# Decoding doubles with a two-slope activation, and a new table of engines and ranks, in an attention-plus-MLP kernel

## The chip, the cores and the metric

The kernel runs on one core of one Trainium2 chip. The metric is the device time of one execution in microseconds; a kernel's time is the median of several runs. In the text PE is TensorE, DVE is VectorE, ACT is ScalarE, POOL is GpSimd and SP is SyncE, whose queue issues all DMAs here.

## The reference

Causal attention over 4 batches, 12 heads, 448 positions and 64 channels; its output, as 1792 rows of 768, goes through a two-layer MLP.

```
scores = np.matmul(q, k.transpose(0, 1, 3, 2)) / np.sqrt(64)
scores = np.where(mask, -1000000000.0, scores)         # mask: above the diagonal
attn = np.exp(scores - np.max(scores, axis=-1, keepdims=True))
attn = attn / (np.sum(attn, axis=-1, keepdims=True) + 1e-09)
x = np.matmul(attn, v).transpose(0, 2, 1, 3).reshape(1792, 768)
h = x @ w_in                                            # w_in 768 x 2048
out = ((h - np.tanh(h)) @ w_out).astype(np.float32)     # w_out 2048 x 768
```

The two weight matrices arrive as 8-byte floats. The result has to be close to what float32 would give, while the matrix products run on 16-bit numbers. So every operand is scaled by a power of two and split into a high and a low float16 half, and each product is made of three: high by high, high by low, low by high.

## The kernel before, in words

**An operation recorded, then placed.** Nothing is issued when it is written. `Engine` hands each operation to `Work.add`, which notes its reads and writes; `Work.schedule` (line 166) then lists all operations in one order, by a rank that each carries (`rank(...)`, from the table `RANK`) and by the planner's own prices, and `Work.emit` issues them. Every instruction of the trace therefore has line 232. Some operations have two or three forms, one for each engine that can do them: `Work.either` takes the engine from a string of the table `CFG`, letter by letter in turn ("AVV": ACT, DVE, DVE, and again). Within an engine the order is fixed when the program is built.

**Front: weights, and the first 128 rows of each batch.** `w_in_chunk` takes one of 8 blocks of 256 columns of `w_in`: two loads of 768 KB, two calls of `decode`, a bound on the magnitudes, and `split` into halves. `decode` makes float32 from an 8-byte float with integer work. ACT multiplies the upper word by 2^-112 into PSUM; a first DVE pass (SCALAR_TENSOR_TENSOR) shifts that left by 3 and ORs in three bits of the lower word, and a second ORs in the sign, which the shift had pushed out. The first pass leaves the magnitude in a scratch buffer of the tile `e`, and the bound is taken from there: for `w_in` by a matmul of those magnitudes with ones, for `w_out` by an ACT instruction Abs whose accumulator sums them. `w_out_half` does the same for two halves of 8 loads each, through two landing buffers. Meanwhile `first_rows` computes the attention of rows 0 to 127 of two batches at a time (chunks `c` and `c2`), and `mlp_g` the first MLP layer for them.

**Attention of the other 320 rows.** `attention(b)` goes over 6 pairs of heads; there are 24 pairs in all. For each pair `prep` loads q and k, takes a bound of each (`bound`, DVE TENSOR_REDUCE), and splits q, k and v into halves. `weights_unit` runs three times: score matmuls (18 for a pair), a DVE custom instruction that adds the mask and finds the row minimum (tile `prob`), ACT Exp, a reciprocal, and `split` of the 5 probability tiles of a pair into `pn` (high, then low); a DMA transposes `pn` to `pt` (three for a pair, one buffer for each of the three). `values` multiplies `pt` with v (54 matmuls), and `split_x` writes the halves of x.

**MLP.** For each block of 128 hidden columns `mlp1` issues 18 matmuls into one of two PSUM banks (`b_m`), ACT Tanh and a DVE subtraction write `t`, and `split` makes `g`. `mlp2` issues 48 matmuls for a block of 128 rows and half the columns, evacuates them to `o` and stores them. The MLP matmuls of a batch are placed between the attention matmuls of the next, so PE has them to fill its time with. What is left when attention ends is PE work alone.

`split` (line 410) is the place where engines trade: the high half is one multiplication (`scaled`: DVE, ACT or POOL), and the low half is one DVE instruction, or two on POOL (multiply in place, subtract).

Of the kernel before, what the change touches and what calls it, by code (L numbers as in the profile page):

```python
# [9 lines left out]
F32 = mybir.dt.float32  # L10
BF16 = mybir.dt.bfloat16
I16 = mybir.dt.int16
I32 = mybir.dt.int32
U16 = mybir.dt.uint16
I64 = mybir.dt.int64
AF = mybir.ActivationFunctionType
ALU = mybir.AluOpType
# [241 lines left out]
def attention_then_mlp(ctx, tc, qk, v, w_in, w_out, out):  # L259
# [13 lines left out]
    V, A, G, T, S = (Engine(wk, n) for n in "VAGTS")  # L273
# [5 lines left out]
    NCC = DM // P  # L279
# [32 lines left out]
    ones = buf([P, P], BF16, "ones")  # L312
# [16 lines left out]
    q16_ring = ring(3, [P, 2, SEQ1], F16, "q16")  # L329
# [67 lines left out]
    def bound(o, i, junk=None, tag=None):  # L397

        if junk is None:
            V.tensor_reduce(o, i, axis=AX.X, op=ALU.max, apply_absolute_value=True)  # L400
            return
        wk.either(tag, lambda: V.tensor_reduce(o, i, axis=AX.X, op=ALU.max, apply_absolute_value=True),
                  lambda: A.activation(junk, i, AF.Abs, accum_out=o))
# [15 lines left out]
    def decode(y, raw, t, tag):  # L419

        words = raw.rearrange("p a b -> p (a b)").bitcast(I32)
        lo, hi = words[:, 0::2], words[:, 1::2]
        yi = y.rearrange("p a b -> p (a b)").bitcast(I32)
        top = words.bitcast(U16)[:, 1::4]
        wk.either("shift" + tag, lambda: V.tensor_scalar(t, lo, 29, None, ALU.logical_shift_right),
                  lambda: A.activation(t, top, AF.Copy, scale=2.0 ** -13, bias=2.0 ** -14 - 0.5),
                  lambda: G.tensor_scalar(t, top, 2.0 ** -13, 2.0 ** -14 - 0.5, ALU.mult, ALU.add))
        for n in range(2):  # L430
            part = slice(n * NW // 2, (n + 1) * NW // 2)
            g = bank_w()[:, :NW // 2]
            A.activation(g, hi.bitcast(F32)[:, part], AF.Copy, scale=2.0 ** -112)
            V.scalar_tensor_tensor(t[:, part], g.bitcast(I32), 3, t[:, part], ALU.logical_shift_left, ALU.bitwise_or)
            V.scalar_tensor_tensor(yi[:, part], g.bitcast(I32), -2 ** 31, t[:, part], ALU.bitwise_and, ALU.bitwise_or)

    def scratch(i, n=4):
        return e_block.bitcast(I32)[:, (i % n) * NW:(i % n + 1) * NW]

    def w_in_chunk(j):  # L440
        y = view(TS[3 + j % 2], 0, [NCC, 256], F32)
        pm = bank_1[:, :256]
        mags = []
        for a in range(2):
            i = 2 * j + a
            t = view(TS[i % 3], 0, [3, 256], I64)
            rank(RANK["c0"] - 1 if i < CFG["early"] else RANK["w_in"])
            S.dma_start(t, w_in[a * 3 * P:(a + 1) * 3 * P, j * 256:(j + 1) * 256].rearrange("(c p) f -> p c f", p=P))
            rank(RANK["w_in"])
            decode(y[:, a * 3:(a + 1) * 3], t, scratch(i), "_in")  # L450

            mag = scratch(i).bitcast(BF16)[:, 1::2].rearrange("p (c f) -> p c f", c=3)
            mags += [mag[:, c] for c in range(3)]
        with wk.group():
            for cc in range(NCC):
                T.matmul(pm, ones, mags[cc], start=(cc == 0), stop=(cc == NCC - 1))
        acc, s = r_acc(), r_s1()
        V.tensor_reduce(acc, pm, axis=AX.X, op=ALU.max)
        scales(us_in[:, j:j + 1], s, acc, 1e-30)
        split(w_in16[j][:, 0], w_in16[j][:, 1], y, s, "w_in")  # L460
# [4 lines left out]
    def w_out_half(n):  # L465

        ys = [view(TS[m], 0, [4, HALF], F32) for m in ((1, 2, 3, 4), (5, 6, 7, 4))[n]]
        to = ([TS[0], TS[1], TS[2], TS[3]], [ES[1], TS[5], TS[6], TS[7]])[n]
        acc = acc_out[n]
        for m in range(4):  # L470
            for a in range(2):
                i = n * 8 + 2 * m + a
                t = view(ES[1 + i % 2], 0, [2, HALF], I64)
                f0 = (2 * m + a) * 2 * P
                S.dma_start(t, w_out[f0:f0 + 2 * P, n * HALF:(n + 1) * HALF].rearrange("(c p) e -> p c e", p=P))
                mag = scratch(i, 2)
                decode(ys[m][:, 2 * a:2 * a + 2], t, mag, "_out")
                A.activation(mag.bitcast(F32), mag.bitcast(F32), AF.Abs, accum_out=acc[:, 2 * m + a:2 * m + a + 1])
        a1, s = r_acc(), r_s1()
        V.tensor_reduce(a1, acc, axis=AX.X, op=ALU.max)  # L480
        bound_scale(us_out[:, n:n + 1], s, a1, 0, mx_w)
        V.tensor_scalar(s_out[n], rel_in, s, None, ALU.mult)
        for m in range(4):
            w_out16[n][m] = view(to[m], 0, [2, 4, HALF], F16)
            for a in range(2):
                part = slice(2 * a, 2 * a + 2)
                split(w_out16[n][m][:, 0, part], w_out16[n][m][:, 1, part], ys[m][:, part], s_out[n][:, 2 * m + a:2 * m + a + 1], "w_out")
# [161 lines left out]
    def prep(b, hp, vf, sv):  # L649

        kq = qk_ring()
        S.dma_start(kq, qk[b, hp, :, P:])
        kf, qf = kq[:, :SEQ], kq[:, SEQ:]
        o = Chunk()
        ma, m2, us, s, o.cn = r_ma(), r_m2(), r_us2(), r_s2(), r_cn()
        bound(ma[:, 0:1], qf)
        bound(ma[:, 1:2], kf)
        with wk.group():
            for i in range(2):
                over_partitions(ma[:, i:i + 1], 2 + i)  # L660
        V.tensor_reduce(m2, bank_1[:, 2 * P:].rearrange("p (i n) -> p i n", i=2), axis=AX.X, op=ALU.max)
        scales(us, s, m2, 1e-12)
        V.tensor_scalar(o.cn, us[:, 0:1], us[:, 1:2], -(D ** -0.5), ALU.mult, ALU.mult)
        o.k, o.q = k16_ring(), q16_ring()
        split(o.k[:, 0], o.k[:, 1], kf, s[:, 1:2], tag(b, "k"))
        split(o.q[:, 0], o.q[:, 1], qf, s[:, 0:1], tag(b, "q"))
        o.v16 = v16_ring()
        split(o.v16[:, 0], o.v16[:, 1], vf, sv, tag(b, "v"))
        return o
# [120 lines left out]
        wk.emit()  # L790


CFG = {"early": 4, "e_bufs": 5, "shift_in": "A", "inverse": "A", "w_in": "VGGG", "w_in_lo": "G", "shift_out": "A", "w_out": "VVG", "w_out_lo": "V", "p0": "G", "p0t": "AAAV", "x0": "AV", "g0": "AG", "g0_lo": "G", "g2": "AAGA", "g2_lo": "G", "g": "AVG", "g_lo": "V", "o": "A", "k_first": "V", "k_first_lo": "VGG", "q_first": "A", "q_first_lo": "GV", "v_first": "GV", "v_first_lo": "VGGG", "p_first": "AVA", "p_first_lo": "V", "k": "G", "k_lo": "G", "q": "VAV", "q_lo": "VG", "v": "V", "v_lo": "VG", "p": "AVV", "p_lo": "V", "x": "V"}
RANK = {"c0": -1.131, "w_in": 0.126, "evac": 5.148, "w_out": 5.279, "c0b": 5.008, "att0": 5.082, "att": -0.403}


_OUTS = [((1792, 768), "float32")]
# [27 lines left out]
```

## Time and profile before

| | |
|---|---|
| median of 3 runs | 637.21 us (636.11 to 638.82) |
| the profiled execution | 637.71 us, span 635.7 us from first to last instruction |
| mean granted clock of PE | 0.97 |
| busy: PE, DVE, ACT, POOL | 572.8, 481.1, 293.8, 231.2 us |

The span and the profiled execution differ by 2.0 us, which lie before the first and behind the last instruction. Busy time is the time in which at least one instruction of the engine runs. PE's is no measure of how full it is, because matmuls overlap each other: how many of them are done in a stretch is the better measure. The same holds in small for DVE, whose instructions begin a little before the one ahead has ended.

### The profile page before, as it was taken

The numbers are of one execution on the slowest core, as the hardware profiler recorded it, in microseconds if no ns is written. First come the engines' busy times: TensorE is split into PE (matmuls) and PEld (weight loads), VectorE is DVE, ScalarE is ACT, GpSimd is POOL, SyncE is SP. The second block draws the span as 40 slices with busy tenths as digits, with TensorE's granted clock in tenths as the row PEclk, the third lists the DMA queues.
The fourth block names the chain that finished last, engine by engine and source line by source line (L and its number), as shares of the span: only waits on it lengthen the run. The fifth ranks groups of instructions, "written<-read, shape, count | busy, mean of one in ns | idle before, by whom it ended". The sixth has DMA issues, their size and how long they took to land.

```text
span 635.7 us, 13502 instructions
## 1 busy us (share of the span) xinstructions
PE 572.8 (90%) x5144; PEld 379.5 (60%) x5144; DVE 481.1 (76%) x1407; ACT 293.8 (46%) x792; POOL 231.2 (36%) x260
## 2 busy tenths in 40 slices
PE   3567759999999987999899999999999999999997
PEld 3345538887555554666466666556656666676664
DVE  3999886998999999999797999991399970244000
ACT  6778869984156544645234444330355430132000
POOL 2579985795322425053243335040043410000000
PEclk9779769999999999999989999999999999999999
DMA  8996166655077864645845364772034351000100
GB/s 280 332 336 194 31 198 202 191 150 208 28 168 152 128 132 104 119 92 84 195 97 124 94 101 94 155 144 50 25 86 67 67 104 35 14 1 1 26 26 25
DMA packets 113665, 74.01 MB, mean 116 GB/s; under 512 B 90048, under 2 KB 99776, under 8 KB 113088
## 3 DMA queue, kind: packets, MB, share of 16 engines
q1 hardware_dynamic: 113600, 73.15, 46.5%
q8 instruction: 40, 0.66, 0.4%
q14 instruction: 25, 0.20, 0.1%
HBM read 45.61 MB, written 5.51 MB: 80 GB/s over the span
## 4 chain that ended last, share of the span: by engine, by line
PE 40%; DVE 37%; DMA 10%; ACT 6%; POOL 3%; issue 3%; SPq 0%; ACTq 0%; POOLq 0%; DVEq 0%
PE b_m L232 36%; DVE pn L232 8%; DVE small L232 7%; DVE prob L232 5%; DMA slot<-in_moe_w_in_dram 5%; DVE t L232 4%; DVE g L232 4%; DVE slot L232 3%; DMA e<-in_v_dram 3%; PE b_x L232 2%; ACT e L232 2%; DVE x L232 2%; PE b_s L232 2%; ACT b_s L232 2%; DVE v L232 1%
## 5 line engine op out<-in xcount | busy, mean ns | idle before, releaser
L232 PE MATMUL b_m<-x,w_in 128*128 128x320 f16 (+1 forms) x1728 | 233.5, 293 | 5.8 <-DVE t L232 4.0
L232 PEld LDWEIGHTS <-w_in 128*128 128x128 f16 x1728 | 167.4, 99 | 65.9 <-issue 16.7
L232 PE MATMUL b_m<-slot,g 128*128 128x384 f16 x1152 | 192.6, 327 | 0.0
L232 PEld LDWEIGHTS <-g 128*128 128x128 f16 x1152 | 111.1, 98 | 74.5 <-issue 3.1
L232 ACT ACTIVATE prob<-prob,small 128x256 f32<-128x256 f32 (+2 forms) x120 | 69.1, 576 | 87.7 <-DVE small L232 87.0
L232 DVE SCALAR_TENSOR_TENSOR t<-b_m,small,t 128x320 f32<-128x320 f32 (+1 forms) x96 | 50.1, 522 | 33.2 <-ACT t L232 33.1
L232 ACT ACTIVATE o<-b_m,small 128x384 f32<-128x384 f32 x28 | 16.1, 575 | 124.1 <-PE b_m L232 124.1
L232 DVE SCALAR_TENSOR_TENSOR pn<-prob,small,pn 128x256 f16<-128x256 f32 (+2 forms) x120 | 71.3, 621 | 0.2 <-ACT pn L232 0.2
L232 ACT ACTIVATE t<-b_m,small 128x320 f32<-128x320 f32 (+1 forms) x96 | 47.9, 499 | 48.4 <-PE b_m L232 44.1
L232 POOL TENSOR_SCALAR g<-t,small 128x320 f16<-128x320 f32 (+1 forms) x29 | 18.3, 630 | 139.9 <-DVE t L232 112.0
L232 DVE CUSTOM_DVE_ANT_0 prob<-b_s,mask,small 128x256 f32<-128x256 f32 (+1 forms) x96 | 50.3, 542 | 23.5 <-PE b_s L232 23.4
L232 PE MATMUL b_s<-k,q 64*128 64x384 f16 (+2 forms) x432 | 45.2, 317 | 12.3 <-DVE small L232 5.0
L232 POOL TENSOR_SCALAR slot<-slot,small 128x448 f32<-128x448 f32 (+3 forms) x37 | 35.8, 968 | 36.3 <-DVE slot L232 13.0
L232 DVE SCALAR_TENSOR_TENSOR g<-t,small,g 128x320 f16<-128x320 f32 x64 | 37.1, 585 | 8.1 <-ACT g L232 3.8
L232 ACT ACTIVATE pn<-prob,small 128x256 f16<-128x256 f32 (+2 forms) x50 | 28.2, 576 | 28.3 <-DVE small L232 27.5
L232 DVE SCALAR_TENSOR_TENSOR e<-b_s,e 128x384 int32<-128x384 int32 x64 | 34.5, 550 | 5.1 <-ACT b_s L232 4.6
L232 PEld LDWEIGHTS <-q 64*128 64x128 f16 (+1 forms) x432 | 18.5, 98 | 32.5 <-issue 20.1
L232 PEld LDWEIGHTS <-v 128*64 128x64 f16 x1296 | 32.4, 113 | 8.1 <-issue 8.1
L232 PE MATMUL b_x<-pt,v 128*64 128x128 f16 (+1 forms) x1296 | 35.6, 213 | 0.5 <-DMA pt<-pn 0.2
L232 DVE SCALAR_TENSOR_TENSOR slot<-b_s,e 128x384 int32<-128x384 int32 x64 | 34.6, 551 | 0.5
L232 DVE TENSOR_SCALAR pn<-prob,small 128x256 f16<-128x256 f32 (+2 forms) x70 | 34.5, 506 | 0.6 <-DMA pt<-pn 0.5
L232 PE MATMUL b_m<-slot,first 128*128 128x384 f16 x192 | 33.4, 326 | 0.0
(96 smaller groups left out, 723.0 us busy)
## 6 DMA issues: line engine op xcount, KB each, us to landing
slot<-in_moe_w_in_dram SPq DMA_DIRECT2D x16, 768.0 KB, 5.8
slot<-in_moe_w_out_dram SPq DMA_DIRECT2D x8, 768.0 KB, 4.8
e<-in_moe_w_out_dram SPq DMA_DIRECT2D x8, 768.0 KB, 4.5
slot<-in_qk_dram SPq DMA_DIRECT2D x16, 384.0 KB, 3.2
e<-in_v_dram SPq DMA_DIRECT2D x3, 1536.0 KB, 7.2
out_dram<-o SPq DMA_DIRECT2D x24, 192.0 KB, 1.9
qk<-in_qk_dram SPq DMA_DIRECT2D x8, 384.0 KB, 3.1
g<-in_qk_dram SPq DMA_DIRECT2D x6, 256.0 KB, 6.9
```

The lines of the kernel that those rows point to most:

```text
L232: getattr(self.eng[o["eng"]], method)(*args, **kw)
```

## The change

Three things change.

1. `decode`: ACT's multiplication by 2^-112 becomes Prelu, which scales negative numbers by a further 2^32. After the left shift by 3 such a number keeps its sign in the top bit. So the second DVE pass is dropped, and the one that stays writes the result itself.
2. Bounds. The magnitudes no longer exist in the scratch buffer. `w_in` gets an ACT Abs over the 1536 decoded columns of a chunk, written as bfloat16 to the buffer that will take the high half, and the matmul with ones reads that. The bound of `w_out` and those of q and k go through `bound`, with engines by turns: `b_out` "AAV", `b_qk` "VVA".
3. `CFG` and `RANK` have new values throughout. The ones that move most: the low half of the probabilities `p_lo` from "V" to "GV", `p` from "AVV" to "VA", `g_lo` from "V" to "GV", `g` from "AVG" to "A", `w_in_lo` from "G" to "V", `k` from "G" to "A", `q` from "VAV" to "AAG", `x` from "V" to "AV".

```diff
@@ decode
-            A.activation(g, hi.bitcast(F32)[:, part], AF.Copy, scale=2.0 ** -112)
-            V.scalar_tensor_tensor(t[:, part], g.bitcast(I32), 3, t[:, part], ALU.logical_shift_left, ALU.bitwise_or)
-            V.scalar_tensor_tensor(yi[:, part], g.bitcast(I32), -2 ** 31, t[:, part], ALU.bitwise_and, ALU.bitwise_or)
+            A.activation(g, hi.bitcast(F32)[:, part], AF.Prelu, scale=2.0 ** -112, alpha=2.0 ** 32)
+            V.scalar_tensor_tensor(yi[:, part], g.bitcast(I32), 3, t[:, part], ALU.logical_shift_left, ALU.bitwise_or)
@@ w_in_chunk
-            mag = scratch(i).bitcast(BF16)[:, 1::2].rearrange("p (c f) -> p c f", c=3)
-            mags += [mag[:, c] for c in range(3)]
+        acc, s = r_acc(), r_s1()
+        mag = w_in16[j][:, 0].bitcast(BF16)
+        A.activation(mag, y, AF.Abs)
+        pm = bank_1[:, :256]
         with wk.group():
             for cc in range(NCC):
-                T.matmul(pm, ones, mags[cc], start=(cc == 0), stop=(cc == NCC - 1))
-        acc, s = r_acc(), r_s1()
+                T.matmul(pm, ones, mag[:, cc], start=(cc == 0), stop=(cc == NCC - 1))
@@ w_out_half
-                A.activation(mag.bitcast(F32), mag.bitcast(F32), AF.Abs, accum_out=acc[:, 2 * m + a:2 * m + a + 1])
+                y = ys[m][:, 2 * a:2 * a + 2].rearrange("p a b -> p (a b)")
+                bound(acc[:, 2 * m + a:2 * m + a + 1], y, mag.bitcast(F32), "b_out")
@@ prep
-        bound(ma[:, 0:1], qf)
-        bound(ma[:, 1:2], kf)
+        o.k, o.q = k16_ring(), q16_ring()
+        bound(ma[:, 0:1], qf, o.q[:, 0].bitcast(BF16), "b_qk")
+        bound(ma[:, 1:2], kf, o.k[:, 0].bitcast(BF16), "b_qk")
...
-        o.k, o.q = k16_ring(), q16_ring()
@@ tables
-CFG = {"early": 4, "e_bufs": 5, "shift_in": "A", "inverse": "A", "w_in": "VGGG", "w_in_lo": "G", "shift_out": "A", "w_out": "VVG", "w_out_lo": "V", "p0": "G", "p0t": "AAAV", "x0": "AV", "g0": "AG", "g0_lo": "G", "g2": "AAGA", "g2_lo": "G", "g": "AVG", "g_lo": "V", "o": "A", "k_first": "V", "k_first_lo": "VGG", "q_first": "A", "q_first_lo": "GV", "v_first": "GV", "v_first_lo": "VGGG", "p_first": "AVA", "p_first_lo": "V", "k": "G", "k_lo": "G", "q": "VAV", "q_lo": "VG", "v": "V", "v_lo": "VG", "p": "AVV", "p_lo": "V", "x": "V"}
-RANK = {"c0": -1.131, "w_in": 0.126, "evac": 5.148, "w_out": 5.279, "c0b": 5.008, "att0": 5.082, "att": -0.403}
+CFG = {"early": 4, "e_bufs": 5, "b_out": "AAV", "b_qk": "VVA", "shift_in": "AGGG", "inverse": "VAAA", "w_in": "G", "w_in_lo": "V", "shift_out": "A", "w_out": "AAV", "w_out_lo": "V", "p0": "G", "p0t": "A", "x0": "A", "g0": "V", "g0_lo": "GVVG", "g2": "GV", "g2_lo": "G", "g": "A", "g_lo": "GV", "o": "VAA", "k_first": "AVV", "k_first_lo": "V", "q_first": "GAAA", "q_first_lo": "V", "v_first": "AGV", "v_first_lo": "GGVV", "p_first": "A", "p_first_lo": "VG", "k": "A", "k_lo": "GGGV", "q": "AAG", "q_lo": "V", "v": "V", "v_lo": "V", "p": "VA", "p_lo": "GV", "x": "AV"}
+RANK = {"c0": -0.453, "w_in": 0.64, "evac": 7.121, "w_out": 7.805, "c0b": 4.125, "att0": 4.883, "att": -1.096}
```

The order of instructions shows three places on which the prediction rests. The first is DVE in the first `w_in` chunk, with `e` the scratch, `slot` the decoded weights and `b_s` the PSUM bank that ACT writes. Before:

```order
L232 SCALAR_TENSOR_TENSOR e_74<-b_s_111,e_74 128x384
L232 SCALAR_TENSOR_TENSOR slot_69<-b_s_111,e_74 128x384
L232 SCALAR_TENSOR_TENSOR e_74<-b_s_112,e_74 128x384
L232 RECIPROCAL small_108<-small_108 128x4
L232 SCALAR_TENSOR_TENSOR slot_69<-b_s_112,e_74 128x384
```

And with the change:

```order
L232 RECIPROCAL small_108<-small_108 128x4
L232 SCALAR_TENSOR_TENSOR slot_69<-b_s_111,e_74 128x384
L232 SCALAR_TENSOR_TENSOR slot_69<-b_s_112,e_74 128x384
L232 RECIPROCAL small_108<-small_108 128x4
L232 SCALAR_TENSOR_TENSOR slot_69<-b_s_111,e_74 128x384
```

The pass into `e` is gone everywhere: 128 passes become 64. The second place is POOL where the attention of the first pairs begins, with `prob` the probabilities, `pn` their halves, and `v`, `q`, `k` the halves of those operands. Before:

```order
L232 TENSOR_SCALAR v_100<-x_85,small_108 128x512
L232 TENSOR_SCALAR x_85<-x_85,small_108 128x512
L232 TENSOR_TENSOR v_100<-x_85,v_100 128x512
L232 TENSOR_SCALAR qk_93<-qk_93,small_108 128x320
L232 TENSOR_TENSOR q_94<-qk_93,q_94 128x320
L232 TENSOR_SCALAR slot_70<-slot_70,small_108 128x448
L232 TENSOR_TENSOR k_98<-slot_70,k_98 128x448
```

And with the change:

```order
L232 TENSOR_SCALAR q_94<-qk_93,small_108 128x320
L232 TENSOR_SCALAR prob_102<-prob_102,small_108 128x256
L232 TENSOR_TENSOR pn_106<-prob_102,pn_106 128x256
L232 TENSOR_SCALAR prob_104<-prob_104,small_108 128x384
L232 TENSOR_TENSOR pn_106<-prob_104,pn_106 128x384
L232 TENSOR_SCALAR prob_101<-prob_101,small_108 128x256
L232 TENSOR_TENSOR pn_106<-prob_101,pn_106 128x256
L232 TENSOR_SCALAR prob_105<-prob_105,small_108 128x448
L232 TENSOR_TENSOR pn_106<-prob_105,pn_106 128x448
```

POOL gets half of the low halves of the probabilities, as pairs of instructions, which it did not touch before. The third place is DVE behind the scores of the last (24th) pair of heads, with `t` the hidden block of the MLP and `x` the attention output. Before:

```order
L232 SCALAR_TENSOR_TENSOR pn_106<-prob_105,small_108,pn_106 128x448
L232 TENSOR_SCALAR x_85<-b_x_113 128x320
L232 SCALAR_TENSOR_TENSOR x_85<-b_x_113,x_85 128x320
L232 TENSOR_SCALAR x_85<-b_x_113 128x320
L232 SCALAR_TENSOR_TENSOR x_85<-b_x_113,x_85 128x320
L232 SCALAR_TENSOR_TENSOR t_88<-b_m_114,small_108,t_88 128x320
```

And with the change:

```order
L232 SCALAR_TENSOR_TENSOR pn_106<-prob_105,small_108,pn_106 128x448
L232 TENSOR_SCALAR small_108<-small_108 128x2
L232 COPY small_108<-small_108 64x2
L232 SCALAR_TENSOR_TENSOR t_87<-b_m_114,small_108,t_87 128x320
L232 SCALAR_TENSOR_TENSOR t_88<-b_m_115,small_108,t_88 128x320
L232 SCALAR_TENSOR_TENSOR g_84<-t_88,small_108,g_84 128x320
L232 SCALAR_TENSOR_TENSOR t_86<-b_m_114,small_108,t_86 128x320
```

With the change the first MLP layer of the third batch stands behind the probabilities of the last pair: 32 blocks `t` follow them, where 16 did. On PE 576 first-layer and 582 second-layer matmuls follow the first scores of the last pair, where it was 306 and 480.

## Rows read from the trace of the kernel before

**Rows 1.** The page: busy us of each engine, and the chain that ended last.
```profile
PE 572.8 (90%) x5144; PEld 379.5 (60%) x5144; DVE 481.1 (76%) x1407; ACT 293.8 (46%) x792; POOL 231.2 (36%) x260
...
PE 40%; DVE 37%; DMA 10%; ACT 6%; POOL 3%; issue 3%; SPq 0%; ACTq 0%; POOLq 0%; DVEq 0%
```

**Rows 2.** Windows by stage: PE, PEld, DVE, ACT, POOL busy (count), clock, DMA share, GB/s.
```profile
20.00:100.00 80.00, 52.20 (x386) 37.63 (x387) 72.18 (x278) 61.98 (x164) 64.48 (x47) 0.79 0.66 214
100.00:176.00 76.00, 74.34 (x600) 57.47 (x598) 69.72 (x130) 47.08 (x100) 50.84 (x71) 1.00 0.48 152
176.00:513.50 337.50, 317.93 (x3239) 200.84 (x3237) 300.76 (x892) 149.67 (x438) 108.12 (x126) 0.99 0.53 108
513.50:635.70 122.20, 118.52 (x868) 76.16 (x866) 28.35 (x65) 21.72 (x46) 3.08 (x6) 1.00 0.10 27
```

**Rows 3.** Windows of two stretches within attention, same columns.
```profile
200.00:240.00 40.00, 36.63 (x436) 21.80 (x433) 39.92 (x129) 21.12 (x63) 12.54 (x14) 1.00 0.75 144
...
420.00:460.00 40.00, 40.00 (x350) 24.67 (x349) 13.66 (x44) 8.98 (x29) 6.09 (x7) 1.00 0.34 68
```

**Rows 4.** Windows behind attention: one with first-layer, one with second-layer matmuls alone.
```profile
560.00:580.00 20.00, 20.00 (x149) 14.40 (x148) 9.93 (x19) 5.90 (x11) 1.59 (x3) 1.00 0.01 2
...
600.00:620.00 20.00, 20.00 (x126) 12.04 (x124) 0.00 (x0) 1.74 (x3) 0.00 (x0) 1.00 0.10 30
```

**Rows 5.** Groups by form (busy us, mean ns; then idle before): decode, and halves of weights.
```profile
L232 DVE SCALAR_TENSOR_TENSOR e<-b_s,e 128x384 int32<-128x384 int32 x64 | 34.5, 550 | 5.1 <-ACT b_s L232 4.6
...
L232 ACT ACTIVATE b_s<-slot 128x384 f32<-128x384 f32 x48 | 24.2, 511 | 3.0 <-DVE slot L232 3.0
...
L232 DVE SCALAR_TENSOR_TENSOR slot<-slot,small,slot 128x768 f16<-128x768 f32 x16 | 18.7, 1189 | 0.0
...
L232 ACT ACTIVATE e<-e 128x768 f32<-128x768 f32 x16 | 13.4, 838 | 2.1 <-DVE slot L232 2.0
```

**Rows 6.** Groups by form, attention and MLP.
```profile
L232 DVE SCALAR_TENSOR_TENSOR g<-t,small,g 128x320 f16<-128x320 f32 x64 | 37.1, 585 | 8.1 <-ACT g L232 3.8 <-POOL g L232 3.7
L232 DVE SCALAR_TENSOR_TENSOR t<-b_m,small,t 128x320 f32<-128x320 f32 x64 | 34.9, 546 | 29.0 <-ACT t L232 29.0
...
L232 DVE SCALAR_TENSOR_TENSOR pn<-prob,small,pn 128x384 f16<-128x384 f32 x48 | 30.9, 667 | 0.0
...
L232 POOL TENSOR_TENSOR k<-slot,k 128x448 f16<-128x448 f32 x16 | 17.3, 1084 | 1.3
...
L232 DVE TENSOR_SCALAR pn<-prob,small 128x384 f16<-128x384 f32 x28 | 16.0, 584 | 0.5 <-DMA pt<-pn 0.5
...
L232 POOL TENSOR_SCALAR slot<-slot,small 128x448 f32<-128x448 f32 x16 | 12.1, 753 | 20.3 <-DVE k L232 11.5 <-DVE small L232 8.0
...
L232 DVE TENSOR_REDUCE small<-slot 128x1 f32<-128x448 f32 x16 | 9.7, 608 | 0.0
```

**Rows 7.** Timeline of DVE: first scores of the first and the last pair.
```profile
175.94 0.47 DVE L232 CUSTOM_DVE_ANT_0 prob<-b_s,mask,small 128x256 f32<-128x256 f32 x1
...
513.44 0.48 DVE L232 CUSTOM_DVE_ANT_0 prob<-b_s,mask,small 128x256 f32<-128x256 f32 x1
513.84 0.08 DVE L232 DVE_READ_ACCUMULATOR2_ANT small<- 128x1 f32 x1
```

**Rows 8.** The chain that ended last (start us, us): matmuls of one pair.
```profile
514.15 0.69 PE b_s L232 x6
...
517.86 1.34 PE b_x L232 x54
```

**Rows 9.** Timelines around 337 us: a DVE instruction, and POOL beside it.
```profile
336.49 1.50 DVE L232 SCALAR_TENSOR_TENSOR pn<-prob,small,pn 128x384 f16<-128x384 f32 x1
...
336.25 1.33 POOL L232 TENSOR_TENSOR v<-e,v 128x512 f16<-128x512 f32 x1
```

**Rows 10.** DMA issues (count, median us to landing), and SP's timeline of two transposes.
```profile
pt<-pn SPq DMA_TRANSPOSE x72, 3.7
...
203.25 2.88 SPq L232 DMA_TRANSPOSE pt<-pn  x2
```

More of the change, by code (lines that the diff above doesn't have):

```diff
@@ L441, in w_in_chunk @@
         y = view(TS[3 + j % 2], 0, [NCC, 256], F32)
-        pm = bank_1[:, :256]
-        mags = []
         for a in range(2):
```

## The prediction

> **What bounds the kernel now.** I read the windows by stage first. There are three stages. In the front, up to the first scores of the 24 head pairs at 176 us [rows 7], DVE is busy 72.2 of 80 us and 69.7 of 76 us [rows 2]. In attention, from there to the first scores of the last pair at 513.4 us [rows 7], DVE is busy 300.8 of 337.5 us. In the tail, 122.2 us, DVE is busy 28 us and PE is full [rows 2]. The chain that ended last says the same: PE and DVE hold 40% and 37% of it [rows 1].
>
> Attention itself alternates. In one stretch DVE is busy 39.92 of 40 us; in another it has 13.7 us to do and PE is busy throughout [rows 3]. PE's order is fixed and holds MLP matmuls between the attention's, so a stretch with many of them is bound by PE and one with few by DVE. What PE can do is read from the tail: 149 first-layer matmuls of 320 columns in 20 us, 0.134 us each, and 126 second-layer ones in 20 us, 0.16 us each [rows 4]. A pair's own matmuls are some 2.9 us: 54 take 1.34 us, and 18 score matmuls, at 0.69 us for 6 with overlap, about 1.6 us [rows 8]. Attention holds 846 first-layer and 708 second-layer matmuls by the order, so PE needs 113 + 113 + 23 x 2.9 = 293 us of these 337.5, and DVE 301. Both are near the whole.
>
> **The change part by part.** A DVE instruction starts 0.08 us before the one ahead ends (0.40 us from start to start at a duration of 0.48 [rows 7]), so one taken away frees its duration less 0.08. The counts are differences of the two orders.
>
> *Front.* 64 decode passes go: 64 x (0.55 - 0.08) = 30.1 us of DVE [rows 5]. Added are 8 low halves of `w_in` of 1536 elements, which POOL did: a pass of 768 takes 1.19 us [rows 5], so I take 2.1 us each, 16 us. The small ones: bounds of `w_out` 5 x 0.86 us, high and low halves of the first 256 rows +11, other halves and evacuations moved off DVE -10 us. The sum is -9 us on 148. ACT gets 8 Abs of 1536 elements (838 ns for 768 [rows 5], so 1.5 us each, 12 us) and loses 12 shifts of 0.9 us to POOL, which is even. POOL loses about 40 us of 118. Prelu is in no trace of before; I price it as the Copy that it replaces, 511 ns [rows 5], and from above as twice that. A new wait stands there: the matmul with ones now waits for an Abs over the whole chunk, 1.5 us, 8 times; it delays that chunk's halves, while DVE decodes the next one. DVE is busy nine tenths of the front, so I pass 6 of the 9 us on; the ends are 0 (loads and ACT set the pace) and -12 (POOL's relief counts too).
>
> *Attention on DVE.* Until the last pair's scores 59 of 115 low halves of probabilities go to POOL: 24 of 384 elements at 0.667 - 0.08 [rows 6], 35 others at about 0.51, 32 us. High halves: 25 fewer at 0.28 to 0.56 us, 11 us. Bounds of q and k: 17 fewer at 0.53 or 0.40, 8 us. MLP: 31 low halves `g` x 0.5, 16 high x 0.36 and 16 `t` x 0.47 [rows 6], 29 us; half of that has merely moved behind the last pair. x and q lose 10 us; low halves of q, k and v, outputs and small ones gain 20. The sum is -70: 301 becomes about 230 us. ACT gains some 31 us on 150, and POOL some 32 on 108.
>
> *Attention on PE.* The order now holds 576 and 618 MLP matmuls in this stage: 77 + 99 + 67 = 243 us.
>
> *Length of the stage.* Neither floor, 230 or 243, is reached, because the two alternate. I went through the 23 intervals between first scores, took DVE's and PE's work in each by these prices from the order, and added up the larger one. For before this gives 333, against 337.5 measured, so the method holds to 1.5%. For the change it gives 251. Several intervals are now under 8 us. There another limit stands: a pair has three transposes, issued 1.44 us apart, landing 3.7 us after issue [rows 10], into single buffers that the 54 matmuls (1.34 us) must have read: 2 x 1.44 + 3.7 + 1.34 = 7.9 us. This adds 7 us, and the 1.5% another 4. I take 263. The ends are 251, and 273 (PE's floor at before's ratio, 243 x 337.5/301).
>
> *Tail.* The 270 first-layer and 102 second-layer matmuls that left the stage above come here: 36 + 16, and one more group of 54, together 54 us; 122 becomes 176. POOL's share of `g` hides: two instructions, about 1.4 us, every other block, against 18 matmuls or 2.4 us a block.
>
> *Sum.* Front -6, attention 263 - 337.5 = -74.5, tail +54: -26.5 us. The profiled execution took 637.7 (2.0 us beyond its span), so 611.2. It is 0.1% above the median, so the forecast is **611**. Its own range, 251 to 273 with the front's 0 to -12, is 593 to 627.
>
> **POOL and DVE together.** While POOL worked on `v` until 337.58, a DVE instruction of 384 elements took 1.50 us instead of about 0.61, and ended 0.4 us behind it [rows 9]. Such collisions are in the means that I used (667 ns). The work that can collide hardly grows: DVE's instructions of this kind (two operands in SBUF, or a high half) fall from about 150 to 100 us in the stage, and POOL's rise from 108 to 140; the product of the two, over the stage's length, goes from 48 to 53. So I add nothing. The Trainium skill (SBUF — State Buffer, "Who interferes with whom") says that the two engines share one pair of ports as an exclusive lock, held for the whole instruction, so that the second one blocks fully. The trace agrees (1.50 us). By that rule 100 + 140 = 240 us could not overlap at all; that is below 263, so the sum would stay, but with only 23 us of room, and it is the reason behind the fourth rival.
>
> **The rivals.**
> 1. *PE alone is the bound.* DVE's relief is enough for the stage to reach 251 and the front -12: 637.7 - 12 - 86.5 + 54 = 593. For it: intervals of 7 to 8 us did occur before. Against it: the margins between DVE and PE are now small in most intervals.
> 2. *Given back in the tail.* The stage comes out at 288, 12.5 us a pair, because ACT, which now makes most high halves, bounds and half of x, delays the Exp behind them in its queue by 1 us a pair. Then 637.7 - 6 - 49.5 + 54 = 636: no change. For it: 54 us are certain to be added behind attention. Against it: ACT would be busy 181 of 263 us, far from full.
> 3. *Prelu is slower than Copy.* At twice the price ACT gets 33 us more in the front, where it is busy 62 of 80 and 47 of 76 us [rows 2]; the front grows by about 12 instead of shrinking by 6: 629.
> 4. *POOL lands on attention's chain: slower.* A low half on POOL takes 0.75 + 1.08 us at 448 elements [rows 6] where DVE needs 0.69, so 1.15 us longer, before the transpose can start, and each may hold up a DVE instruction by 0.9 us [rows 9], say 0.4 on average. With 2.5 of them a pair that is 3.8 us on top of DVE's 10.0: 13.8 x 23 = 317, and 637.7 - 6 - 20.5 + 54 = **665**. It decides from 12.6 us a pair on, that is if each costs more than 1 us net. Against it: five probability buffers let POOL work on one tile while DVE does the next.
>
> **How the numbers follow.** Chances: the forecast 0.60, rival 1 0.15, rival 2 0.09, rival 3 0.05, rival 4 0.11. The range leaves out rival 4 and part of rival 1: 594 to 636. A measurement of this kernel tells about 0.5%, 3.2 us, from no change. Faster by more than that: the forecast but for its edge, rivals 1 and 3, 0.80. Within it: rival 2, 0.09. Slower: rival 4, 0.11.
>
> **What would show it.** Right: DVE busy near 410 us, ACT near 345, POOL near 255; first scores near 170 us; the last pair's first scores near 433; 176 us from there with PE full; 64 decode passes of 0.55 us, and Prelu near 0.51. Wrong: more than 12.6 us a pair between first scores; POOL as releaser of DVE or of the transposes; DVE's low halves well above 0.67 us; a Prelu far above 0.51; or PE idle in the tail.

## The result, and the profile after

The changed kernel takes 607.69 us (median of 4 runs, 606.72 to 608.92) against 638.01 us for the kernel before on the same chip (4 runs): a ratio of 0.953, 95% interval 0.950 to 0.956. It is faster by 30.3 us; 26.5 were forecast. The predicted 611 us lie 3.3 us above the median, which is inside the predicted range of 594 to 636. The profiled execution took 606.7 us with a span of 605.0, 30.7 less than before.

The page of the changed kernel, busy time and the chain that ended last, as in [rows 1]:

```profile
PE 566.0 (94%) x5144; PEld 377.8 (62%) x5144; DVE 430.2 (71%) x1250; ACT 346.6 (57%) x884; POOL 256.0 (42%) x327
...
PE 48%; DVE 28%; ACT 10%; DMA 6%; issue 5%; POOL 1%; SPq 0%; DVEq 0%; ACTq 0%; POOLq 0%
```

Its windows by stage, with the columns of [rows 2] (length, PE, PEld, DVE, ACT, POOL busy, clock, DMA share, GB/s):

```profile
20.00:100.00 80.00, 60.80 (x486) 46.47 (x484) 73.53 (x263) 67.22 (x171) 41.36 (x40) 0.94 0.70 224
100.00:164.00 64.00, 61.52 (x487) 46.46 (x486) 58.38 (x112) 41.92 (x79) 37.18 (x51) 1.00 0.54 170
164.00:424.00 260.00, 255.94 (x2801) 160.04 (x2798) 245.63 (x745) 177.55 (x500) 142.84 (x183) 1.00 0.66 133
424.00:605.00 181.00, 177.35 (x1324) 116.71 (x1321) 42.67 (x86) 46.34 (x93) 28.20 (x42) 1.00 0.11 26
```

The stages are cut where DVE takes up the first scores of the first and of the last pair, as in [rows 7]. DVE's timeline in the changed kernel:

```profile
164.00 0.48 DVE L232 CUSTOM_DVE_ANT_0 prob<-b_s,mask,small 128x256 f32<-128x256 f32 x1 [0.41 <-PE b_s L232]
...
424.00 0.48 DVE L232 CUSTOM_DVE_ANT_0 prob<-b_s,mask,small 128x256 f32<-128x256 f32 x1
```

| stage | before | after | difference | forecast |
|---|---|---|---|---|
| front, to the first pair's scores | 175.9 | 164.0 | -11.9 | -6 |
| attention, to the last pair's scores | 337.5 | 260.0 | -77.5 | -74.5 |
| tail | 122.2 | 181.0 | +58.8 | +54 |

The tail is full of matmuls: windows of the changed kernel with first-layer and with second-layer matmuls alone show 150 and 125 in 20 us, nearly the counts of [rows 4] (149 and 126).

```profile
520.00:540.00 20.00, 20.00 (x150) 14.39 (x148) 6.62 (x12) 8.73 (x17) 5.64 (x10) 1.00 0.00 1
...
560.00:580.00 20.00, 20.00 (x125) 12.05 (x124) 0.62 (x1) 1.16 (x2) 0.00 (x0) 1.00 0.11 30
```

The groups by form give the prices of the new operations. With [rows 5 and 6]: a decode pass 547 ns (550 before), Prelu 514 and 519 (Copy: 511), the Abs of a chunk 1476, the low half of a chunk 1986, a shift on POOL 1122; and a low half of 384 probabilities 728 on DVE (667 before), or 730 + 1013 on POOL.

```profile
L232 DVE SCALAR_TENSOR_TENSOR slot<-b_s,e 128x384 int32<-128x384 int32 x64 | 34.3, 547 | 5.6 <-ACT b_s L232 5.3
...
L232 ACT ACTIVATE b_s<-slot 128x384 f32<-128x384 f32 x48 | 24.1, 514 | 3.2 <-DVE slot L232 2.9 <-DMA slot<-in_moe_w_in_dram 0.2
...
L232 POOL TENSOR_TENSOR pn<-prob,pn 128x384 f16<-128x384 f32 x24 | 24.3, 1013 | 2.0
...
L232 POOL TENSOR_SCALAR prob<-prob,small 128x384 f32<-128x384 f32 x24 | 17.5, 730 | 22.8 <-DVE pn L232 10.0 <-ACT x L232 5.7 <-DVE small L232 4.3
L232 DVE SCALAR_TENSOR_TENSOR pn<-prob,small,pn 128x384 f16<-128x384 f32 x24 | 17.5, 728 | 0.2 <-ACT pn L232 0.2
...
L232 DVE SCALAR_TENSOR_TENSOR w_in<-slot,small,w_in 128x1536 f16<-128x1536 f32 x8 | 15.9, 1986 | 0.5 <-POOL w_in L232 0.5
...
L232 ACT ACTIVATE w_in<-slot 128x1536 bf16<-128x1536 f32 x8 | 11.8, 1476 | 0.0
```

### The profile page after: what moved, and what is told of

It is laid out like the page before. It is cut to its first block, busy times and chain, and to the rows that moved or that the text cites. A ratio compares the mean times of both kernels' runs of the same rounds, so it can differ in the third digit from the quotient of the medians.

```text
span 605.0 us, 13701 instructions
## 1 busy us (share of the span) xinstructions
PE 566.0 (94%) x5144; PEld 377.8 (62%) x5144; DVE 430.2 (71%) x1250; ACT 346.6 (57%) x884; POOL 256.0 (42%) x327
## 4 chain that ended last, share of the span: by engine, by line
PE 48%; DVE 28%; ACT 10%; DMA 6%; issue 5%; POOL 1%; SPq 0%; DVEq 0%; ACTq 0%; POOLq 0%
PE b_m L232 41%; DVE small L232 7%; DVE prob L232 4%; DVE pn L232 4%; DVE slot L232 4%; PE b_s L232 3%; DMA e<-in_moe_w_out_dram 3%; PE b_x L232 3%; ACT e L232 2%; DVE v L232 2%; ACT pn L232 2%; ACT b_s L232 2%; DVE t L232 2%; DVE x L232 2%; DVE w_in L232 1%
## 5 line engine op out<-in xcount | busy, mean ns | idle before, releaser
L232 PEld LDWEIGHTS <-g 128*128 128x128 f16 x1152 | 110.4, 98 | 74.5 <-issue 4.5
L232 POOL TENSOR_SCALAR t<-t,small 128x320 f32<-128x320 f32 (+1 forms) x56 | 32.0, 571 | 131.2 <-ACT g L232 108.1
L232 POOL TENSOR_SCALAR prob<-prob,small 128x256 f32<-128x256 f32 (+2 forms) x60 | 40.0, 666 | 90.2 <-ACT pn L232 33.6
L232 DVE TENSOR_SCALAR o<-b_m,small 128x384 f32<-128x384 f32 x10 | 6.1, 612 | 73.6 <-PE b_m L232 73.6
L232 POOL TENSOR_TENSOR pn<-prob,pn 128x256 f16<-128x256 f32 (+2 forms) x60 | 53.4, 890 | 5.0
L232 ACT ACTIVATE pn<-prob,small 128x256 f16<-128x256 f32 (+2 forms) x75 | 41.4, 573 | 23.0 <-DMA pt<-pn 9.8
L232 ACT ACTIVATE g<-t,small 128x320 f16<-128x320 f32 x64 | 35.7, 558 | 29.7 <-DVE t L232 29.5
L232 ACT ACTIVATE o<-b_m,small 128x384 f32<-128x384 f32 x18 | 10.4, 577 | 71.1 <-PE b_m L232 71.1
L232 DVE SCALAR_TENSOR_TENSOR pn<-prob,small,pn 128x256 f16<-128x256 f32 (+2 forms) x60 | 41.3, 692 | 3.1 <-ACT pn L232 3.1
L232 DVE TENSOR_SCALAR small<-small 128x1 f32<-128x1 f32 (+5 forms) x180 | 33.8, 205 | 7.6 <-ACT o L232 6.0
L232 POOL TENSOR_TENSOR g<-t,g 128x320 f16<-128x320 f32 (+1 forms) x40 | 32.7, 818 | 3.3
## 6 DMA issues: line engine op xcount, KB each, us to landing
g<-in_qk_dram SPq DMA_DIRECT2D x6, 256.0 KB, 6.5
```

The costliest lines, as they stand in the source:

```text
L232: getattr(self.eng[o["eng"]], method)(*args, **kw)
```

## The experiments

Twelve kernels ran. Their ratios are to the kernel before, which ran beside them with medians of 636.2 to 636.9 us. In the runs "in its own order" the planner sees the changed tables and writes the same order as in the changed kernel; only then do the named operations take another engine, in the place that they have in that order:

```diff
+SWAP = {"p_lo": "V"}
+def swapped(o):
+    tag, n = o.get("tag", ("", 0))
+    if tag in SWAP:
+        o["eng"] = SWAP[tag][n % len(SWAP[tag])]
+    return o
@@ emit
-            o = self.ops[i]
+            o = swapped(self.ops[i])
```

**1. The code without the tables.** The new `decode` and bounds, with `CFG` and `RANK` of before:

```diff
-CFG = {"early": 4, "e_bufs": 5, "b_out": "AAV", "b_qk": "VVA", "shift_in": "AGGG", ...
-RANK = {"c0": -0.453, "w_in": 0.64, ...
+CFG = {"early": 4, "e_bufs": 5, "b_out": "A", "b_qk": "V", "shift_in": "A", ...
+RANK = {"c0": -1.131, "w_in": 0.126, ...
```

> The new decode and bounds with the tables of before (bounds of w_out all on ACT, of q and k all on DVE, as before). Theory A, that the decode relieves DVE in the front alone and the tables do the rest: first scores come 10 to 20 us earlier than 176 (DVE loses 30 us of 142 there), the attention stage keeps its 337 and the tail its 122, so 618 to 628 us. Rival, that the saved decode passes are what the whole gain comes from: near 608. Rival, that the front is set by loads and ACT: 633 to 640.

637.87 us, ratio 1.002 (0.999 to 1.005): nothing. First scores at 175.7 us, where they were at 175.9, though DVE lost its 64 passes. Its window of the front:

```profile
20.00:100.00 80.00, 50.80 (x385) 37.32 (x384) 57.38 (x240) 73.32 (x182) 63.88 (x47) 0.83 0.71 227
```

DVE is busy 57.4 of 80 us instead of 72.2 [rows 2], and ACT 73.3 instead of 62.0: it now makes the Abs of `w_in` too. The time is the one of the second rival (633 to 640); its cause, loads and ACT, is not shown by that. The decode itself did become faster. Its groups before, in this run and with the change give shortest, median and longest in ns, then the first and the last start:

```profile
L232 DVE SCALAR_TENSOR_TENSOR slot<-b_s,e x64: 526/551/559, 13.1 to 147.4; 128x384 int32<-128x384 int32 x64
...
L232 DVE SCALAR_TENSOR_TENSOR slot<-b_s,e x64: 524/548/559, 12.5 to 138.4; 128x384 int32<-128x384 int32 x64
...
L232 DVE SCALAR_TENSOR_TENSOR slot<-b_s,e x64: 520/547/558, 12.1 to 138.2; 128x384 int32<-128x384 int32 x64
```

The last pass starts 9 us earlier than before, as early as with the whole change. The first scores did not follow, because PE has its MLP matmuls to work off first. In the kernel before, the chain that ended last runs through them from 141 us on, with hardly a gap until the first scores (`b_s`):

```profile
141.11 8.99 PE b_m L232 x78
...
150.16 14.62 PE b_m L232 x90
...
167.06 7.80 PE b_m L232 x48
174.86 0.92 PE b_s L232 x12
```

In this run the chain has 108 of them in a row, until 167.0 us, and then DVE's halves of v and k:

```profile
151.20 15.79 PE b_m L232 x108
```

By 100 us PE has done 154 MLP matmuls before, 148 here and 251 with the change. So the relief reached the decode and not PE. What holds PE back there was not tried apart. Open are ACT's fuller queue, POOL (busy 63.9 of 80 us, as before), and PE's granted clock, which goes between 1.2 and 2.4 GHz: from 60 to 100 us its mean is 0.74 before and here, with PE busy 27 of the 40 us, and 0.92 with the change, with PE busy 35.

**2. The tables without the code.** The old `decode` and bounds, with the new `CFG` and `RANK` (the exchange of run 1, the other way round).

> The old decode and bounds with the new tables. Theory A: attention stage near 265 and tail near 178, as with the whole change (-17 us for the two), and a front that is 10 to 20 us longer than with the whole change, so 618 to 630 us. Rival, that the tables only pay when the passes are gone: 637 or more. Rival, that the tables are all of it: near 608.

640.04 us, ratio 1.006 (1.003 to 1.008): slightly slower. The first pair's scores come at 171.2 us, 7.2 later than with the whole change, but the second pair's not before 199.3, 26 us later than there (173.2); I had expected 10 to 20. From the second pair's scores to the last pair's (456.2) it takes 256.9 us, near the 250.8 of the changed kernel, and the tail takes 180.7. So theory A had the later stages right and the front too short, and the time is the one of the first rival (637 or more). Neither half of the change is worth anything by itself; both together are worth 30 us.

**3. The pass put back.** The changed kernel in its own order, with a second DVE pass behind each of the 64 (the planner prices the two as one, so that the order stays):

```diff
+            with wk.group():
                 V.scalar_tensor_tensor(yi[:, part], g.bitcast(I32), 3, t[:, part], ALU.logical_shift_left, ALU.bitwise_or)
+                V.scalar_tensor_tensor(yi[:, part], g.bitcast(I32), -2 ** 31, yi[:, part], ALU.bitwise_and, ALU.bitwise_or)
```

> The changed kernel in its own order, with 64 second DVE passes put back behind the decode passes (the sign is ORed in once more, which changes nothing). It adds 64 x 0.47 = 30 us of DVE work in the front. Theory A, DVE sets the front's pace: first scores 18 to 30 us later, 625 to 638 us. Rival, that the front became shorter through POOL's relief or PE's earlier MLP work: less than 8 us later, 608 to 616.

634.86 us, ratio 0.998 (0.995 to 1.000). First scores at 191.8 us, 27.8 later, for 30 us of work, as theory A expected; the last decode pass starts 27.3 us later (165.5 instead of 138.2). The stages behind it are those of the changed kernel, 260.5 and 180.9 us. Its windows of the rest of the front and of attention:

```profile
100.00:191.80 91.80, 80.44 (x621) 61.02 (x623) 87.17 (x174) 57.55 (x108) 40.09 (x57) 0.96 0.52 159
191.80:452.30 260.50, 256.24 (x2802) 160.37 (x2799) 245.56 (x744) 177.69 (x500) 144.68 (x183) 1.00 0.66 133
```

So with the new tables the front passes on nearly all that is added to DVE.

**4. `w_in`'s low halves on POOL.** In its own order, `SWAP = {"w_in_lo": "G"}`.

> The changed kernel in its own order, but the 8 low halves of the first weights go to POOL again, as before the change. DVE loses 8 x 1.99 = 16 us of its 142 in the front, POOL gains some 37. Theory A, DVE alone sets the front's pace, as the pass put back showed: first scores 7 to 14 us earlier, 594 to 601 us. Rival C, that POOL's relief was what made the front 12 us shorter and not 6: first scores no earlier or later, 607 us or more.

622.40 us, ratio 0.978 (0.975 to 0.981): theory A failed. The time is in rival C's range, 607 or more, which put no size on the delay. First scores at 179.4 us, 15.4 later, though DVE has less to do. The window of the front:

```profile
20.00:100.00 80.00, 53.78 (x369) 39.14 (x370) 50.77 (x229) 57.24 (x150) 70.28 (x49) 0.85 0.58 185
```

A line of the waits from 20 to 80 us gives what waited, for what, us in total, how often, and the longest:

```profile
DVE slot L232 <- POOL w_in L232: 12.2, 5, 3.1
```

DVE is busy 50.8 us of 80 (73.5 in the change), and POOL 70.3 (41.4). Five decode passes wait for POOL, 12.2 us in all: the decoded columns lie in two buffers, and a chunk's buffer is free again only when POOL has subtracted from it. POOL's timeline, of this run:

```profile
61.70 1.54 POOL L232 TENSOR_SCALAR w_in<-slot,small 128x1536 f16<-128x1536 f32 x1
63.33 0.92 POOL L232 TENSOR_SCALAR e<-slot 128x768 int32<-128x768 uint16 x1
64.33 1.04 POOL L232 TENSOR_TENSOR pn<-pn,small 128x512 f32<-128x512 f32 x1
65.47 1.54 POOL L232 TENSOR_SCALAR slot<-slot,small 128x1536 f32<-128x1536 f32 x1
67.10 3.10 POOL L232 TENSOR_TENSOR w_in<-slot,w_in 128x1536 f16<-128x1536 f32 x1
```

And of the kernel before:

```profile
63.03 1.55 POOL L232 TENSOR_SCALAR w_in<-slot,small 128x1536 f16<-128x1536 f32 x1
64.54 1.04 POOL L232 TENSOR_TENSOR pn<-pn,small 128x512 f32<-128x512 f32 x1
65.56 1.55 POOL L232 TENSOR_SCALAR slot<-slot,small 128x1536 f32<-128x1536 f32 x1
67.19 3.10 POOL L232 TENSOR_TENSOR w_in<-slot,w_in 128x1536 f16<-128x1536 f32 x1
70.27 1.55 POOL L232 TENSOR_SCALAR w_in<-slot,small 128x1536 f16<-128x1536 f32 x1
```

One chunk cost POOL 7.24 us there (63.03 to 70.27) with hardly a gap, 1.04 of them for the first rows' attention. POOL's eight subtractions began 8.1 us apart on average (26.0 to 82.9 us), so it had little room left before the change. In this run it has more to do than then: 12 shifts and all eight high halves are its own too.

**5. The shifts of `w_in` on ACT.** In its own order, `SWAP = {"shift_in": "A"}`.

> The changed kernel in its own order, but the 12 shifts that POOL makes for the first weights go to ACT again, as before: ACT gains 12 x 0.93 = 11 us in the front. Theory A, DVE alone sets the front's pace: 605 to 611 us. Rival D, that ACT is as full as DVE there (with the tables of before it was busy 73 of 80 us): first scores 6 to 12 us later, 613 to 620 us.

612.72 us, ratio 0.963 (0.960 to 0.965), first scores at 169.5 us, 5.5 later: between the two expectations, just below rival D's. Its window of the front has ACT at 72.0 of 80 us (67.2 in the change) and DVE at 70.8:

```profile
20.00:100.00 80.00, 58.91 (x452) 43.83 (x450) 70.79 (x255) 72.03 (x178) 27.58 (x28) 0.85 0.67 214
```

Half of the 11 us come out as time, although POOL is relieved of the same shifts (27.6 us busy instead of 41.4). ACT is as full as DVE here.

**6. Low halves of the probabilities on DVE.** In its own order, `SWAP = {"p_lo": "V"}`.

> The changed kernel in its own order, but the 45 low halves of probabilities that POOL makes in batches 1 to 3 go to DVE at the same places. DVE gains 45 x 0.52 = 23 us of work and loses some 12 us of waiting for the ports. Theory A, DVE is still near the bound in attention (245.6 us busy of 260.0): the attention stage grows by 8 to 23 us, 615 to 630 us. Rival, POOL's late halves and its port collisions cost more than they relieve: the stage shrinks, 595 to 605 us.

609.85 us, ratio 0.958 (0.952 to 0.964). The attention stage takes 261.9 us, 1.9 more; neither expectation held. Its window:

```profile
165.00:426.90 261.90, 255.91 (x2799) 160.21 (x2796) 253.09 (x785) 178.12 (x500) 82.88 (x102) 1.00 0.66 132
```

DVE does 41 low halves more in this stage, and POOL is busy 60 us less, yet DVE's busy time rises by 7.5 us alone (245.6 to 253.1). The groups by form tell why. In the whole kernel DVE's busy time rises by 7.6 us (430.2 to 437.8), the low halves as such take 19.9 us more (26.1 + 20.4 + 14.9 us for 105 instructions, against 17.5 + 14.3 + 9.7 for 60), and the others became shorter: the high half of 384 took 526 ns beside POOL's work in the change, and 416 here. The two rows of this run:

```profile
L232 DVE SCALAR_TENSOR_TENSOR pn<-prob,small,pn 128x384 f16<-128x384 f32 x42 | 26.1, 638 | 0.0
...
L232 DVE TENSOR_SCALAR pn<-prob,small 128x384 f16<-128x384 f32 x18 | 7.5, 416 | 1.0 <-DMA pt<-pn 1.0
```

**7. All low halves of the probabilities on POOL.** In its own order, `SWAP = {"p_lo": "G"}`.

> The changed kernel in its own order, but all 90 low halves of probabilities of batches 1 to 3 are made by POOL, 45 more than in the change. If POOL's work cost DVE nothing, DVE would lose 23 us; with the share that the run with these halves on DVE showed (45 of them moved DVE's busy time by 7.5 us) it loses about 8. Theory A, ports: DVE busy in the stage falls by 5 to 10 us only, the time stays within 605 to 613. Rival 4, POOL lands on attention's chain once it makes nearly all of them: 620 us or more. Rival, POOL's work runs beside DVE's: 595 to 603.

621.36 us, ratio 0.975 (0.972 to 0.979): rival 4 held, and my own expectation failed. The stage takes 273.0 us, though DVE's busy time falls by 13.8. Its window:

```profile
166.10:439.10 273.00, 260.34 (x2804) 161.62 (x2801) 231.80 (x704) 178.96 (x502) 202.28 (x265) 0.99 0.62 127
```

A line of the waits in this stage:

```profile
DVE prob L232 <- POOL pn L232: 22.1, 22, 2.5
```

And the same line for the changed kernel:

```profile
DVE prob L232 <- POOL pn L232: 3.9, 5, 1.1
```

DVE's next masked scores wait for one of the five probability buffers, which POOL still reads: 22 times instead of 5. With none, 45 and 90 of the 90 low halves of batches 1 to 3 on POOL the stage takes 261.9, 260.0 and 273.0 us. Making all of them on POOL is clearly worse than half. Half and none can't be told apart: the intervals of their ratios, 0.950 to 0.956 and 0.952 to 0.964, overlap.

**8. The engines of before in the order of the change.** In its own order, q, k, v, `p`, x, `g` and the bounds of q and k as before:

```diff
+SWAP = {"k": "G", "k_lo": "G", "q": "VAV", "q_lo": "VG", "v": "V", "v_lo": "VG", "p": "AVV", "p_lo": "V", "x": "V", "g": "AVG", "g_lo": "V", ..., "b_qk": "V"}
```

> The changed kernel in its own order, ranks and front, but the engines that split q, k, v, the probabilities, x and g, and the bounds of q and k, are those of before (so 45 + 14 low halves of probabilities, 25 high ones, 16 bounds, 32 g and 12 x come back to DVE, and some low halves of q, k and v go to POOL). Theory A, that DVE's relief by the new engines made the attention stage short: DVE gains about 53 us of work there less some 10 of collisions, on 245.6 us of 260, so the stage takes 295 to 315 us and the time 640 to 660. Rival B, that the new order of the matmuls did it (288 first-layer matmuls moved behind the attention): below 623 us.

644.46 us, ratio 1.011 (1.007 to 1.015), and 36.1 of the 38.1 us that the span is longer lie in the attention stage, as theory A expected. The order was planned for the other engines, so a part of the 36.1 may be due to that. DVE is at 284.9 of its 296.1 us:

```profile
165.70:461.80 296.10, 262.90 (x2800) 161.43 (x2795) 284.89 (x863) 135.66 (x390) 101.11 (x118) 0.99 0.57 117
```

**9 and 10. Parts of that.** In its own order, `SWAP = {"g": "AVG", "g_lo": "V"}` for the first run; `SWAP = {"p": "AVV", "p_first": "AVA", "b_qk": "V"}` for the second.

> The changed kernel in its own order, but the halves of g of the last three quarters of the rows are split by the engines of before (high halves by ACT, DVE, POOL in turn, low halves all on DVE). In the attention stage DVE gains 16 low halves x 0.5 and 10 high ones x 0.36 = 12 us. Theory A, DVE's work is what counts there: the stage grows by 6 to 12 us, 613 to 620 us. Rival, MLP work is only filler and its engines do not matter: 606 to 610.

615.98 us, ratio 0.968 (0.964 to 0.972). The stage is 269.3 us long, 9.3 more; DVE's busy time in it is 10.4 us more (256.1).

> The changed kernel in its own order, but the high halves of the probabilities are split by the engines of before (ACT, DVE, DVE; it was DVE, ACT), and the bounds of q and k are all on DVE. DVE gains some 11 + 8 = 19 us in the attention stage and ACT loses about as much. Theory A, DVE's work is what counts there: the stage grows by 10 to 19 us, 617 to 627 us. Rival, ACT is as full in the pairs as DVE: 606 to 612.

617.87 us, ratio 0.969 (0.965 to 0.974). The stage is 270.3 us long, 10.3 more; DVE is busy 14.9 us more (260.5). In both runs theory A held. With the 1.9 of run 6 these parts make 21.5 of the 36.1 us by which run 8 lengthens the stage. The rest lies with q, k, v and x, or in the parts together; that was not tried apart.

**11. The order.** The changed kernel, planned with the `RANK` of before.

> The changed kernel with all its engines, but with the ranks of before, so that the planner writes another order. Theory A, that the engines made the gain: 600 to 616 us, wherever the MLP matmuls stand. Rival B, that the order made it: 622 us or more.

609.58 us, ratio 0.957 (0.954 to 0.960): theory A held, and it can't be told from the change. But its stages are quite different. Windows of attention and tail:

```profile
163.50:477.60 314.10, 308.58 (x3215) 196.79 (x3212) 259.15 (x776) 191.30 (x532) 157.17 (x201) 1.00 0.57 113
477.60:605.80 128.20, 124.58 (x910) 80.24 (x908) 25.35 (x56) 28.42 (x60) 16.37 (x24) 0.99 0.11 28
```

Attention takes 314.1 us and the tail 128.2, with 838 first-layer and 720 second-layer matmuls in the stage: by the prediction's prices 112 + 115 + 67 = 294 us of PE work, and 20 us in which PE lacked some. In the change that rest is 260.0 - 243 = 17 us, and before it was about 40 (the trace has 864 and 721 matmuls in the 337.5 us: 298). That 288 matmuls moved behind the attention is worth nothing; that PE lacks less work in the stage is worth 23 us. Run 1 has the same code and the same `RANK` as this run, so the two differ in `CFG` alone (and in what order the planner makes of it): the new engines are worth 28 us, with first scores 12.1 us earlier (163.5 against 175.7), a stage 22.1 shorter and a tail 6 longer.

**12. More shifts on POOL.** An attempt to go below the change: in its own order, `SWAP = {"shift_in": "G", "shift_out": "AG"}`.

> The changed kernel in its own order, with the last 4 of the shifts of the first weights and half of the 16 of the second weights moved from ACT to POOL: ACT loses 12 x 0.93 = 11 us in the front, POOL gains 12 x 1.12 = 13 us. If ACT's share of the front's pace goes on as the run with the shifts on ACT showed (12 of them cost 5.5 us): first scores up to 3 us earlier, 604 to 607. Rival, POOL's lateness and its ports take that back: 608 to 614 us.

608.24 us, ratio 0.955 (0.952 to 0.959), first scores at 164.8 us: the rival held, nothing gained. No run here is faster than the change.

## Why the prediction came out

**The sum held, and a part of that is luck.** The front came out 5.9 us better than its term, attention 3.0 better and the tail 4.8 worse. Attention was forecast at 263 us and took 260.0, of which PE's matmuls are 243. The method (the larger of DVE's and PE's work in each interval) stands: worked out again with DVE's measured busy time and PE's matmuls from the trace at the prediction's prices, it gives 252 of the 260.0 us, and 329 of 337.5 before. But two of its terms did not hold. DVE was forecast at 230 us in the stage and was busy 245.6. And the 7 us for transposes rest on a limit of 7.9 us for a pair, while five of the 23 intervals between first scores are shorter, 5.9 to 7.2 us; so no run shows that this limit lengthened the stage. One of the five, in DVE's timeline of the changed kernel:

```profile
297.40 0.47 DVE L232 CUSTOM_DVE_ANT_0 prob<-b_s,mask,small 128x256 f32<-128x256 f32 x1
...
303.86 0.46 DVE L232 CUSTOM_DVE_ANT_0 prob<-b_s,mask,small 128x256 f32<-128x256 f32 x1
```

Two slips change little: 251 + 7 + 4 is 262, and the upper end, called PE's floor, was scaled with DVE's 301 us; with PE's 293 it is 280 instead of 273. Runs 8 to 10 show that DVE's relief made the stage shorter, and run 11 that the new order is not needed for it.

**The front: -6 forecast, -11.9 measured.** The step that was mis-sized is "I pass 6 of the 9 us on". The work was right: DVE's busy time to the first scores fell by 10.1 us (152.0, where the prediction has 148, to 141.9), ACT's stayed (122.4 and 122.7), POOL's fell by 35 where I had 40. By the trace all of the 9 came through: the last decode pass starts 9.2 us earlier. Another 1.9 us may be PE's, where 48 second-layer matmuls stand before the first scores instead of 60. The prediction read the front as DVE's alone. But in the second of [rows 2] PE is busy 74.3 of 76 us and DVE 69.7, and the last 34 us of the chain ahead of the first scores are PE's (run 1). With the new engines, in the change and in runs 3 to 12, the first scores come 25.6 to 26.3 us after the last decode pass, so there the first scores follow the decode, and what holds it up comes out as time: 27.8 us for DVE's passes (run 3), 15.4 for the low halves on POOL (run 4), 5.5 for the shifts on ACT (run 5). These are prices in the changed kernel and not parts of the 11.9, because runs 3 and 4 give DVE and POOL more than they had before the change. Three engines take turns at each chunk through two buffers, and each of them holds up the others when it gets more. Why the code alone gained nothing stays open (run 1). The clock does not settle it: with a mean of 0.87 from 20 to 100 us, runs 9 and 11 have their first scores at 163.9 and 163.5 us, as early as the change with 0.94.

**The tail: +54 forecast, +58.8 measured.** The prices hold. The count was off: by the trace, 288 first-layer and 467 second-layer matmuls stood behind the last pair's scores before, not 306 and 480, since PE had gone on by the time DVE took the scores up. With 576 and 580 after, the difference is 288 x 0.134 + 113 x 0.16 + 1.34 = 58.0 us. What the tail gained, the attention stage lost, so this error and part of the other are one.

**"POOL and DVE together: I add nothing" was wrong.** DVE was forecast busy near 410 us and was 430.2. The largest item of my DVE sum, 32 us for low halves moved to POOL, is worth a third of that: run 6 moves 41 of them back (22 us at my prices), and DVE's busy time in the stage changes by 7.5 us. Some 10 of the other 14 us are DVE's remaining instructions, which get shorter without POOL's beside them. Two that collided, in DVE's timeline of the changed kernel:

```profile
236.08 0.92 DVE L232 TENSOR_SCALAR pn<-prob,small 128x384 f16<-128x384 f32 x1
...
238.11 1.26 DVE L232 SCALAR_TENSOR_TENSOR pn<-prob,small,pn 128x384 f16<-128x384 f32 x1
```

POOL's timeline of the same stretch:

```profile
235.74 1.04 POOL L232 TENSOR_TENSOR k<-slot,k 128x448 f16<-128x448 f32 x1
237.17 0.74 POOL L232 TENSOR_SCALAR prob<-prob,small 128x384 f32<-128x384 f32 x1 [0.39 <-DVE pn L232]
237.99 0.96 POOL L232 TENSOR_TENSOR pn<-prob,pn 128x384 f16<-128x384 f32 x1
```

A high half of 384 takes 0.92 us where run 6 has a mean of 0.416, and a low half 1.26 where the prediction took about 0.61: each stands beside a POOL instruction that began just before. The first met k's low half, which POOL made before the change as well, the second one of the instructions that POOL took over. By the product of the two engines' busy times, which I used, little should have changed; but the instructions that POOL took over sit in the same place of the pair as DVE's of the same kind, and the product does not see that (argued from these rows, not tried apart). The Trainium skill (SBUF — State Buffer, "Who interferes with whom") says that a DVE instruction with two inputs in SBUF and a GpSimd one that reads SBUF contend, and that the second blocks fully. The trace agrees: the low half took 1.26 us and ended 0.42 us after POOL's.

**The rivals.** Rival 1 (593) needed the front at its end of -12, which came, and attention at 251, which did not. Rival 2 (636) needed a stage of 288 us; it took 260.0, with ACT busy 177.6. Rival 3 fell: Prelu takes 514 ns against 511 for Copy. The Trainium skill (ScalarE: Activation LUTs, "What ACT_TABLE_LOAD costs") states one element per cycle at 1.2 GHz, 0.833 ns, for every function. The trace agrees, with 0.835 ns an element between Prelu's 514 ns for 384 and the 1476 ns of Abs for 1536. Rival 4 (665) did not decide here, at 260.0 / 23 = 11.3 us a pair against the 12.6 that I set, and POOL's chain claims 1% of the span. But run 7 shows it at work one step further on, at 273.0 us. Of the signs of being wrong that I had named, two came up weakly: DVE's low halves at 728 ns instead of 667, and POOL as what DVE waited for, 3.9 us in all (run 7).

## What to carry to other kernels

Where several engines hand a piece of work round through few buffers, count all of them against each other, and with them the engine that uses the result, here PE: a cheaper operation and a new division of the work were each worth nothing here, and together 30 us. When work goes from DVE to POOL, price it by what DVE's busy time really loses (a third of the nominal here), and stop before POOL holds the buffers that DVE waits for. The lengths of stages only say where matmuls stand; compare the time in which PE lacks work instead.

## What the runs showed of the hardware

Prelu with two slopes costs ACT what Copy costs (514 against 511 ns for 384 elements), and both kernels load one activation table in all. A subtraction of 1536 elements on POOL takes 3.10 us, and DVE's one-pass form of the whole low half 1.99 us on average. Taking 45 low halves from POOL to DVE raised DVE's busy time by 7.6 us in the whole kernel and lowered POOL's by 67.1 (256.0 to 188.9).
